# Layer 3 of a fused attention and MLP kernel: another order of its seven products, and 16 weight blocks decoded inside it

## The chip, the cores and the metric

The kernel runs on one core of one Trainium2 chip. The metric is device time in microseconds (us) of one execution.

## The reference

Three parts follow each other. The attention has 4 batches, 12 heads, 448 positions and a head size of 64, and its scores go through a capped tanh. The first MLP takes the largest of three products and multiplies it by an output matrix, all 768 wide. The second, of which the change treats the first half ("layer 3" below), is a gated product of width 1536:

```python
def _moe2_ref(x, w_gate, w_val, w_out) -> np.ndarray:
    gate = 1.0 / (1.0 + np.exp(-(x @ w_gate)))
    val = x @ w_val
    return (gate * val @ w_out).astype(np.float32)

def reference(**kwargs):
    ...
    attn_out = _attn_ref(**attn_kwargs)
    B, H, S, D = attn_out.shape
    x = np.ascontiguousarray(attn_out.transpose(0, 2, 1, 3)).reshape(B * S, H * D)
    x = _moe_ref(x=x, **moe_kwargs)
    return _moe2_ref(x=x, **moe2_kwargs)
```

The weights arrive as 8-byte floats.

## The kernel before

All weights have to be decoded from 8 bytes to 4. `decode` does this with one ScalarE operation (the absolute value of the high word) and four of VectorE: two `tensor_scalar` with one tensor operand, two `scalar_tensor_tensor` with two. A product in full precision is made of products of rounded parts: weights and inputs are split into a high and a low part (a ScalarE copy and a VectorE subtraction), and high x high, high x low and low x high are added up in PSUM.

The program runs in five stages. In the attention, 24 head pairs run one after the other (`Pair`, 6 per batch), by an order written out by hand (`PROGRAM`), in which letters also stand for steps of other work: "P", "W" and "O" advance layer 1, "d" one step of `decode_ahead`. That is a generator over 48 weight blocks (`later_weights`) with three steps a block: load 768 KB from the input and take Abs, two VectorE operations, two more and a store of 384 KB to DRAM (`ws`, `wso`, `ws3`). The blocks stand in the order in which they are used: 18 of w1, w2, w3, 6 of the output matrix, then 24 of gate and val, the blocks 10 and 11 first, then 0 to 9. What is left of layer 1 (72 products in all) and layer 2 (24) follow; they advance the decoding too, until the list is empty.

Layer 3 (`Layer3`) multiplies in the seven-product way of Strassen and Winograd: a pair of weight blocks (2j, 2j+1) and a pair of sequences give seven products, numbered 1 to 7, instead of eight. A quad (k) is one such weight pair, of gate (m = 0) or val (m = 1), for one or both of the two sequence pairs: quads 0, 1, 12 and 13 have one pair, 2 to 11 have both. Each product is 9 matmuls. `load` fetches a quad's two decoded blocks from `ws3` into `wf[k]`; `prepare`, two products ahead (AHEAD), forms sums of the weights at product 6 (four VectorE operations), and splits each weight into a ring of three places. `run` walks through the quads in `ORDER`; `ONTO` says which product goes on adding in the bank of an earlier one. `after` takes the results out: 1 is copied by ScalarE, and 6, 7, 5, 4, 3 are VectorE adds. `out` applies the sigmoid on ScalarE for a gate, or multiplies with the gate on VectorE and stores 224 KB to `us` for a val. The intermediate results live in chunks of a free list (`free`): 6 from the start and 6 more from hook (1, 5).

`hooks` are called behind product i of quad k: early ones form inputs for the second sequence pair, and from quad 2 to 11, four in each quad, `step` advances `last_weights`: rows of the last matrix are loaded (768 KB) and decoded into a tile, stored to `ws2`, loaded back as `formed` with both halves, summed in `form` (four operations) and stored to `wt2`. The last hooks fetch blocks of `us` into rooms whose old contents are no longer used, and load the first weights of layer 4 (`weights(0)`, tile w2a, three loads, the third of which takes a place of the ring). Layer 4 multiplies them. The order of instructions on each engine and queue outside the attention is set by a planner that goes by the program's order and by when it expects operands; SP issues nearly all DMAs, in one queue.

## Time and profile before

| | us |
| --- | --- |
| median of 3 runs | 1015.9 |
| the runs | 1015.47, 1015.9, 1018.31 |
| the profiled execution | 1020.39 |
| its span | 1018.5 |

A profile is one execution. It gives the busy time of each engine: PE is TensorE's matmuls, PEld its weight loads, DVE VectorE, ACT ScalarE, POOL GpSimd, SP the engine that issues DMAs. Matmuls overlap, so a full PE may still run at different paces. A name such as "ring<-w" says which tile is written from which, L541 is line 541 of the kernel, x52 a count. "<-" behind idle time names what ended it.

In the profile, times are us from the start of the span. The attention with its part of layer 1 takes the first 380 us, layer 1 and 2 run on to 551, layer 3 to 857 and layer 4 to the end.

### The profile page before, as it was taken

The page shows a single profiled execution, that of the slowest core. Times are in us where ns is not written, and L with a number is a line of the kernel's source. Part 1 is how long each engine was busy: PE and PEld are TensorE (multiplying, and loading weights), DVE is VectorE, ACT ScalarE, POOL GpSimd, SP SyncE. Part 2 cuts the span into 40 slices and gives each one's busy share as a digit, 9 for nine tenths or more (in the row PEclk, how much of TensorE's full clock was granted, in tenths as well). Part 3 has the DMA queues.
Part 4 walks back from the last instruction along what each step waited for, and adds up shares of the span by engine and source line. Part 5 has one row for each costly group of instructions (what it writes and reads, how often), then busy time and mean ns, then how long its engine had stood idle before and what let it go on. Part 6 is the DMA issues. An engine that isn't in the chain of part 4 may idle for free.

```text
span 1018.5 us, 13734 instructions
## 1 busy us (share of the span) xinstructions
PE 1001.9 (98%) x5048; PEld 837.1 (82%) x5048; DVE 753.5 (74%) x1136; ACT 500.4 (49%) x707; POOL 39.5 (4%) x49
## 2 busy tenths in 40 slices
PE   8999998999999999999999999999999999999997
PEld 3336666777788779999999999999999999999997
DVE  3988899887888886876537877686766479975661
ACT  7886676766667653444435432423241334443330
POOL 1000000000000000003630000000000000000000
PEclk9999999999999999999999999999999999999999
DMA  6774788676564569776215445454543267521331
GB/s 208 248 215 157 273 278 269 213 238 186 183 212 155 176 218 321 265 265 215 91 48 171 160 151 181 144 173 163 180 157 135 77 209 268 190 86 48 88 113 60
DMA packets 93340, 183.06 MB, mean 180 GB/s; under 512 B 33232, under 2 KB 60752, under 8 KB 92752
## 3 DMA queue, kind: packets, MB, share of 16 engines
q1 hardware_dynamic: 92832, 181.77, 53.4%
q8 instruction: 42, 0.69, 0.3%
q10 hardware_dynamic: 432, 0.33, 0.1%
q14 instruction: 34, 0.28, 0.1%
HBM read 134.48 MB, written 47.58 MB: 179 GB/s over the span
## 4 chain that ended last, share of the span: by engine, by line
PE 85%; DVE 6%; DMA 4%; ACT 3%; issue 1%; SPq 0%; DVEq 0%; ACTq 0%
PE mm L561 30%; PE mm L188 29%; PE mm L694 15%; PE pv L346 5%; PE sc L308 4%; DMA wf<-ws 1%; ACT e L313 1%; PE rest L305 1%; DMA wraw<-in_moe_w_dram 1%; ACT e L327 1%; DVE wd L131 1%; DVE wd L132 1%; PE pv L353 1%; PE pv L359 1%; DMA w2a<-ws 1%
## 5 line engine op out<-in xcount | busy, mean ns | idle before, releaser
L561 PE MATMUL mm<-part,ring 128*128 128x448 f32 x1512 | 307.4, 365 | 0.2
L561 PEld LDWEIGHTS mm<-part,ring 128*128 128x128 f32 x1512 | 283.7, 188 | 23.7 <-issue 0.9
L188 PE MATMUL mm<-x,wh 128*128 128x448 f32 x864 | 191.2, 370 | 4.8 <-ACT wh L141 4.8
L188 PEld LDWEIGHTS mm<-x,wh 128*128 128x128 f32 x864 | 161.2, 189 | 27.7 <-ACT wh L141 7.0
L188 PE MATMUL mm<-x,wl 128*128 128x448 f32 x432 | 100.3, 367 | 0.0
L141 ACT CAST wh<-wf 128x768 fp32r<-128x768 f32 x84 | 69.6, 831 | 42.3 <-DMA wf<-ws 24.0
L694 PE MATMUL mm<-w2a,u 128*128 128x384 f32 x504 | 88.5, 334 | 0.2 <-ACT w2a L668 0.2
L694 PEld LDWEIGHTS mm<-w2a,u 128*128 128x128 f32 x504 | 87.5, 188 | 0.6 <-ACT w2a L668 0.6
L188 PEld LDWEIGHTS mm<-x,wl 128*128 128x128 f32 x432 | 81.7, 189 | 7.1
L327 ACT ACTIVATE e<-e,capb 128x448 f32<-128x448 f32 (+1 forms) x96 | 86.1, 948 | 0.7
L313 ACT ACTIVATE e<-sc,tsc 128x896 f32<-128x896 f32 x72 | 70.2, 1007 | 23.3 <-PE sc L308 23.3
L142 DVE TENSOR_TENSOR wl<-wf,wh 128x768 fp32r<-128x768 f32 x72 | 68.5, 954 | 17.4 <-ACT wh L141 16.5
L694 PE MATMUL mm<-w2b,u 128*128 128x384 f32 x378 | 66.0, 334 | 0.0
L694 PEld LDWEIGHTS mm<-w2b,u 128*128 128x128 f32 x378 | 65.6, 188 | 0.0
L188 PE MATMUL mm<-h,wh 128*128 128x448 f32 x288 | 63.4, 368 | 0.0
L540 ACT CAST ring<-w 128x384 fp32r<-128x384 f32 x56 | 28.6, 510 | 69.7 <-PE mm L561 66.6
L678 ACT CAST u<-u 128x1344 fp32r<-128x1344 f32 x24 | 31.7, 1323 | 60.5 <-PE mm L694 53.0
L346 PE MATMUL pv<-e,vs 128*64 128x448 f32 x288 | 59.4, 548 | 0.0
L188 PEld LDWEIGHTS mm<-h,wh 128*128 128x128 f32 x288 | 54.1, 188 | 5.5
L126 ACT ACTIVATE wd<-wraw 128x768 f32<-128x768 f32 x48 | 43.2, 907 | 23.1 <-DMA wraw<-in_moe_w_dram 9.2
L540 ACT CAST ring<-s 128x384 fp32r<-128x384 f32 x42 | 21.5, 513 | 62.2 <-PE mm L561 59.0
L679 DVE TENSOR_TENSOR u<-u,u 128x1344 fp32r<-128x1344 f32 x24 | 37.1, 1552 | 16.6 <-ACT u L678 16.6
(132 smaller groups left out, 1208.7 us busy)
## 6 DMA issues: line engine op xcount, KB each, us to landing
wf<-ws SPq DMA_DIRECT2D x72, 384.0 KB, 3.7
ws<-wd SPq DMA_DIRECT2D x54, 384.0 KB, 2.7
wraw<-in_moe_w_dram SPq DMA_DIRECT2D x18, 768.0 KB, 5.4
wraw<-in_moe_w_out_dram SPq DMA_DIRECT2D x18, 768.0 KB, 4.8
w<-ws SPq DMA_DIRECT2D x28, 384.0 KB, 3.2
us<-temps SPq DMA_DIRECT2D x48, 224.0 KB, 2.0
u<-us SPq DMA_DIRECT2D x8, 1344.0 KB, 7.0
wraw<-in_moe_w_gate_dram SPq DMA_DIRECT2D x12, 768.0 KB, 5.6
```

What stands on the lines that cost most here:

```text
L126: nc.scalar.activation(t, high.bitcast(F32), AF.Abs)
L141: nc.scalar.copy(wh, wf)
L142: (sub or nc.gpsimd.tensor_sub)(wl, wf, f(wh))
L188: nc.tensor.matmul(ps, a[:, c, :], at(x, m, c), start=(n == 0), stop=(n == len(passes) - 1))
L308: nc.tensor.matmul(sc[:, j, :S], kk[own, c * P : (c + 1) * P], qq[own], start=(m == 0), stop=(m == last))
L313: nc.scalar.activation(e, sc[:, :w, :S], AF.Tanh, scale=tsc)
L327: nc.scalar.activation(e, e, AF.Exp, scale=1.0 if self.general else capb)
L346: nc.tensor.matmul(self.pv[0][own, :S], lhs, e, start=(c == 0), stop=(c is None))
L540: nc.scalar.copy(w[:, 0], src)
L561: nc.tensor.matmul(ps, w[:, wm, c, :], x[:, xm, c, :], start=(q == 0 and not onto), stop=(q == len(order) - 1), skip_group_check=bool(onto),)
L679: nc.vector.tensor_sub(self.part[h][1][:, :, cols], src[:, own], f(high))
L694: nc.tensor.matmul(ps, a, ww[g][:, w], start=(c == 0 and m == 0), stop=(c == KC - 1 and m == 2))
```

## The change

Three things change in layer 3, and one tuple in the attention.

- The order of the seven products becomes 1, 2, 6, 5, 7, 3, 4. Products 6, 7 and 4 go on adding in the bank of product 1, and 3 in that of 5. ScalarE copies the bank's state behind 1, 6 and 5; VectorE adds behind 2, 7 and 3; the result of 4 is read from the bank.
- Of gate and val only the blocks 10, 11, 0 and 1 (`BEFORE`) stay in the list that is decoded ahead. The 16 others are decoded inside layer 3, in halves of 384 columns, straight into the tiles from which the ring is filled, during the quad before their own. Their loads from `ws3` fall away, and so do the stores to it.
- The last weights are decoded in halves as well, into the tile in which they are summed; it is stored to `ws2` but not read back. In quads 2 to 11 seven places (three in quads 2 and 11) each take one job. Raw halves come into two places, one of which is a part of the room that gave 6 chunks to the free list and gives 4 now.
- In the attention, `self.whole` is asked where `self.alone` was. The tuple ONESX holds the pairs 0 to 5, and `alone` holds for n < 6.

```diff
+    ONESX = (0, 1, 2, 3, 4, 5)
+    BEFORE = (10, 11, 0, 1)
...
-        ORDER = (1, 6, 7, 2, 5, 4, 3)
-        ONTO = {2: 1, 3: 5}
+        ORDER = (1, 2, 6, 5, 7, 3, 4)
+        ONTO = {6: 1, 7: 1, 4: 1, 3: 5}
...
                     t = self.wpool.tile([P, KC, P], F32, tag=tag, name="w3", bufs=2)
-                    nc.sync.dma_start(out=t, in_=ws3[m, 2 * j + e])
+                    if 2 * j in BEFORE:
+                        nc.sync.dma_start(out=t, in_=ws3[m, 2 * j + e])
...
-                        ps = self.open.pop((p, onto))
+                        ps = self.open[p, onto]
...
-            if i == 1:
-                c[12] = self.new()
-                nc.scalar.copy(c[12], ps)
-            elif i == 6:
-                add(c[12], ps, c[12])
-            elif i == 7:
-                c[21] = self.new()
-                add(c[21], ps, c[12])
-            elif i == 2:
-                self.out(k, p, 0, ps)
-            elif i == 5:
-                t = self.new()
-                add(t, ps, c[21])
-                self.out(k, p, 3, t, t)
+            if i in (1, 6, 5):
+                c[i] = self.new()
+                nc.scalar.copy(c[i], ps)
             elif i == 4:
-                add(c[21], ps, c[21])
-                self.out(k, p, 2, c[21], c[21])
-            elif i == 3:
-                add(c[12], ps, c[12])
-                self.out(k, p, 1, c[12], c[12])
+                self.out(k, p, 2, ps)
+            else:
+                n, block = {2: (1, 0), 7: (5, 3), 3: (6, 1)}[i]
+                add(c[n], ps, c[n])
+                self.out(k, p, block, c[n], c[n])
...
-            for j in (*range(NF - 2, NF), *range(NF - 2)):
+            for j in BEFORE:
                 later_weights += [(cols(w, j), [P, KC, P], ws3[m, j]) for m, w in enumerate((wg, wv))]
...
+        class Decoding:
...
+            def load(self):
+                if self.begun < len(self.decodings):
+                    n = self.decodings[self.begun]
+                    raw = self.places[self.begun % 2]
+                    nc.sync.dma_start(out=raw.rearrange("p c t -> p (c t)"), in_=self.todo[n][0].bitcast(I32))
+                    self.raws[n] = raw
+                    self.begun += 1
...
+            def step(self):
+                n = self.n
+                self.n += 1
+                src, to = self.todo[n]
+                if src is None:
+                    to()
+                    return
+                decode(self.size(n), self.raws.pop(n), False)
+                self.load()
+                if n in self.sums:
+                    self.sums[n]()
...
+        def rows(c, e, h):
+            r = c + e * KC
+
+            def to():
+                if e == h == 0:
+                    formed.append(one_of(wpool, "wraw", 0, [P, 4, HALF], F32, "formed"))
+                return formed[-1][:, 2 * e + h]
+
+            return wo2[r * P : (r + 1) * P, h * HALF : (h + 1) * HALF], to
...
+        for c in range(KC):
+            last_jobs += [(rows(c, e, h), keep(c, e) if h else None) for e in range(2) for h in range(2)]
+            last_jobs.append(((None, lambda c=c: l4.form(c, formed[-1])), None))
+        for k in range(2, end - 1):
+            j, m, _ = l3.quads[k + 1]
+            now = []
+            if 2 * j not in BEFORE:
+                for e in range(2):
+                    for h in range(2):
+                        own = slice(h * HC, (h + 1) * HC)
+                        src = half((wg, wv)[m][2 * j + e][:, own])
+                        now.append(((src, lambda k=k, e=e, own=own: l3.wf[k + 1][e][:, own]), None))
+            places = [0, 1, 2, 3, 4, 5, 6] if now else [1, 3, 5]
+            now += last_jobs[:3]
+            last_jobs = last_jobs[3:]
...
+                plan.append((k, l3.ORDER[place]))
...
-            ((1, 5), lambda: [build(4, y3[:, ends], 1), l3.free.extend(temps(0))]),
-            *(((k, i), step) for k in range(2, end - 1) for i in (1, 7, 5, 3)),
+            ((1, 5), lambda: [build(4, y3[:, ends], 1), begin_decoding()]),
+            *((at, work.step) for at in plan),
```

## Rows read from the trace of the kernel before

**Rows 1.** the page: busy us, share of the span and instructions of an engine

```profile
PE 1001.9 (98%) x5048; PEld 837.1 (82%) x5048; DVE 753.5 (74%) x1136; ACT 500.4 (49%) x707; POOL 39.5 (4%) x49
```

**Rows 2.** busy time of PE, PEld, DVE, ACT, POOL by stage; granted clock, DMA

```profile
0.00:210.00 210.00, 200.65 (x945) 112.51 (x946) 175.21 (x267) 161.44 (x205) 3.25 (x25) 0.99 0.71 231
369.00:420.50 51.50, 51.50 (x255) 44.95 (x253) 39.46 (x57) 19.89 (x29) 0.00 (x0) 1.00 0.78 266
420.50:551.00 130.50, 130.50 (x632) 118.50 (x632) 80.51 (x113) 55.27 (x89) 36.27 (x24) 1.00 0.50 171
551.00:576.50 25.50, 25.38 (x125) 22.84 (x124) 25.43 (x52) 15.50 (x31) 0.00 (x0) 1.00 0.41 143
602.00:806.40 204.40, 204.40 (x1010) 189.40 (x1010) 141.09 (x252) 61.31 (x113) 0.00 (x0) 1.00 0.44 152
```

**Rows 3.** timeline (start, us, engine, line), TensorE, starts of products about 420 us

```profile
413.14 2.60 PE L188 MATMUL mm<-x,wh 128*128 128x448 f32 x12
416.79 2.59 PE L188 MATMUL mm<-x,wh 128*128 128x448 f32 x12
424.39 2.64 PE L188 MATMUL mm<-x,wh 128*128 128x448 f32 x12
428.12 2.64 PE L188 MATMUL mm<-x,wh 128*128 128x448 f32 x12
```

**Rows 4.** timeline, all engines, about 420 us; idle time before in brackets

```profile
417.70 0.96 DVE L131 SCALAR_TENSOR_TENSOR wd<-wraw,wd 128x768 int32<-128x768 int32 x1
418.57 0.61 DVE L430 TENSOR_TENSOR hm<-mm,hm 128x448 f32<-128x448 f32 x1
420.58 2.35 PEld L188 LDWEIGHTS mm<-x,wh 128*128 128x128 f32 x12 [0.36 <-ACT wh L141]
```

**Rows 5.** timeline, TensorE, the first products of layer 3

```profile
550.87 49.48 PE L561 MATMUL mm<-part,ring 128*128 128x448 f32 x240
```

**Rows 6.** line L126, 345 to 560 us: ns min/median/max, first and last start

```profile
L126 ACT ACTIVATE wd<-wraw x17: 892/910/924, 345.1 to 484.1; 128x768 f32<-128x768 f32 x17
```

**Rows 7.** groups by line of layer 3: busy us, mean ns, idle before it

```profile
L541 DVE TENSOR_TENSOR ring<-w,ring 128x384 fp32r<-128x384 f32 x52 | 28.6, 549 | 12.2 <-PE mm L561 9.5 <-ACT ring L540 2.6
L582 DVE TENSOR_TENSOR temps<-mm,temps 128x448 f32<-128x448 f32 x23 | 14.3, 623 | 20.7 <-PE mm L561 20.6
L580 ACT COPY temps<-mm 128x448 f32<-128x448 f32 x23 | 12.2, 533 | 10.9 <-PE mm L561 10.2
L102 DVE SCALAR_TENSOR_TENSOR wd<-wraw,wd 128x768 int32<-128x768 int32 x10 | 9.5, 955 | 0.2
L100 DVE TENSOR_SCALAR wd<-wd 128x768 f32<-128x768 f32 x10 | 5.6, 556 | 4.4 <-ACT wd L99 4.4
```

**Rows 8.** timeline, VectorE, in the first quad of layer 3

```profile
561.55 0.61 DVE L590 TENSOR_TENSOR temps<-mm,temps 128x448 f32<-128x448 f32 x1
```

**Rows 9.** the same view, whole run: a one-operand operation of 448 elements

```profile
L379 DVE CAST x<-xn 128x448 fp32r<-128x448 f32 x6 | 2.3, 387 | 0.0
```

**Rows 10.** timeline, VectorE, two operations that don't depend on each other

```profile
680.06 0.55 DVE L541 TENSOR_TENSOR ring<-w,ring 128x384 fp32r<-128x384 f32 x1
680.53 0.61 DVE L607 TENSOR_TENSOR temps<-temps 128x448 f32<-128x448 f32 x1
```

**Rows 11.** loads of w (384 KB) in layer 3, by tile: issue to landing

```profile
DMA to landing us min/median/max: 2.9/3.2/6.5
```

**Rows 12.** timeline, SP's queue, into layer 4

```profile
837.17 0.37 SPq L667 DMA_DIRECT2D w2a<-ws  x1
849.06 2.18 SPq L626 DMA_DIRECT2D u<-us  x2
```

**Rows 13.** DMA issues: stores of the sums, KB each, us to landing

```profile
wt<-formed SPq DMA_DIRECT2D x6, 768.0 KB, 3.9
```

**Rows 14.** chain that ended last, in order of time (start, us), into layer 4

```profile
854.57 7.23 DMA w2a<-ws
```

**Rows 15.** timeline, TensorE, into layer 4; idle time before in brackets

```profile
862.71 12.60 PE L694 MATMUL mm<-w2a,u 128*128 128x384 f32 x71 [0.25 <-ACT w2a L668]
```

More of the change, by code (lines that the diff above doesn't have):

```diff
@@ L283, in __init__ @@
             self.alone = n < NP and not general
+            self.whole = n in ONESX and not general
             self.own = general
@@ L332, in add_up @@
             nc.vector.tensor_add(self.sum, self.sum, self.e[2])
-            if self.alone:
+            if self.whole:
                 return
@@ L350, in total @@
             ld, wk, ep, pp, mm, (ident, ones, onesx, capb, tsc, kfs, vss, vts) = self.pools
[L351 to L359 removed]
+            if self.alone:
+                self.pv.append(mm.tile([P, 512], F32, tag="mm", name="pv"))
+            for j, own in enumerate(HALVES):
+                if self.whole:
+                    nc.tensor.matmul(self.pv[1][own, :S], onesx[:, j], self.e[None][:, 0], start=True, stop=False)
+            for j, own in enumerate(HALVES):
+                nc.tensor.matmul(self.pv[1][own, :S], ones[:, own], self.sum[:, j], start=not self.whole, stop=True)
         def finish(self):
@@ L626, in fetch @@
             nc.sync.dma_start(out=t, in_=us[self.pairs[e][i], half * KC : (half + 1) * KC].rearrange("c p s -> p c s"))
-        def load_sums(self, c):
-            t = two(self.wpool, "wraw", [P, 4, HALF], F32, "formed")
-            for e in range(2):
-                nc.sync.dma_start(out=t[:, 2 * e : 2 * e + 2], in_=ws2[e * KC + c].rearrange("p (a f) -> p a f", a=2))
-            return t
         def form(self, c, t):
@@ L970, in compute @@
         l4 = Layer4(pairs, rooms, mm, wpool, sm)
-        def last_weights():
-            for c in range(KC):
-                for r in (c, KC + c):
-                    raw = raw_bits(wpool, wo2[r * P : (r + 1) * P, :], [P, DM])
-                    yield
-                    wf = decode(two(wpool, "wf", [P, DM], F32, "wd"), raw)
-                    nc.sync.dma_start(out=ws2[r], in_=wf)
-                    yield
-                t = l4.load_sums(c)
-                yield
-                l4.form(c, t)
-                yield
@@ L986, in compute, with __init__, start, size @@
-        steps = last_weights()
         tops, ends = slice(0, HC), slice(HC, KC)
         end = len(l3.quads) - 1
-        def step():
-            next(steps, None)
+        class Decoding:
+            def __init__(self, todo, sums):
+                self.todo, self.sums, self.raws, self.begun = todo, sums, {}, 0
+                self.decodings = [n for n, (src, _) in enumerate(todo) if src is not None]
+            def load(self):
[5 more added lines that the diff above has]
+                    self.begun += 1
+            def start(self, places):
+                self.places, self.n, self.early = places, 0, None
+                self.load()
+                self.load()
+            def size(self, n):
+                to = self.todo[n][1]()
+                to = to.rearrange("p c f -> p (c f)") if len(to.shape) == 3 else to
+                nc.scalar.activation(to, self.raws[n][..., 1].bitcast(F32), AF.Abs)
+                return to
+            def step(self):
[6 more added lines that the diff above has]
+                decode(self.size(n), self.raws.pop(n), False)
+                self.load()
+                if n in self.sums:
+                    self.sums[n]()
@@ new lines, in half, with keep, store @@
+        def half(src):
+            return src.rearrange("p c f -> p (c f)")
+        formed = []
+        def rows(c, e, h):
[5 more added lines that the diff above has]
+            return wo2[r * P : (r + 1) * P, h * HALF : (h + 1) * HALF], to
+        def keep(c, e):
+            def store():
+                nc.sync.dma_start(out=ws2[c + e * KC].rearrange("p (a f) -> p a f", a=2), in_=formed[-1][:, 2 * e : 2 * e + 2])
+            return store
@@ new lines, in compute @@
+        todo, plan, sums, last_jobs = [], [], {}, []
+        for c in range(KC):
[13 more added lines that the diff above has]
+            last_jobs = last_jobs[3:]
+            for place, (job, done) in zip(places, now):
+                if done:
+                    sums[len(todo)] = done
+                todo.append(job)
+                plan.append((k, l3.ORDER[place]))
@@ L993, in compute, with begin_decoding @@
+        work = Decoding(todo, sums)
+        def begin_decoding():
+            t = rooms.chunks(0, "temps")
+            l3.free.extend(t[:, c] for c in range(HC + 1))
+            size = 2 * HALF
+            spare = t[:, HC + 1 :].rearrange("p c s -> p (c s)")[:, :size]
+            other = one_of(wpool, "wf", 0, [P, size], F32, "raw")
+            work.start([x.bitcast(I32).rearrange("p (c t) -> p c t", t=2) for x in (other, spare)])
         at_ = [
```

9 lines of the change are left out of this document (removed).

## The prediction

> **What bounds the kernel now.** I read the page's busy shares first, then the busy time by stage, then TensorE's own timeline where the change works. TensorE is busy 98% of the span, VectorE 74% [rows 1]. By stage [rows 2] the only stretch in which TensorE is not full is the first 210 us, the attention that comes before most of layer 1: 200.65 of 210. From there to the end TensorE is full: 130.50 of 130.50 in the end of layer 1 and layer 2, 204.40 of 204.40 in the eight middle quads of layer 3. Busy TensorE is not yet TensorE at its peak, so I looked at its pace, which the starts of its products show: a product of layer 1 or 2 is 18 matmuls, and from start to start it takes 416.79 - 413.14 = 3.65 us before 420 us, and 428.12 - 424.39 = 3.73 us after [rows 3]. The clock is granted in full on both sides [rows 2]. The slower pace begins with a gap: at 420.58 the weights of the next product are late by 0.36 us, because a VectorE operation that they stand behind (L430) ran behind a decode operation, L131 [rows 4], and it lasts to the first product of layer 3 at 550.87 [rows 5]. So TensorE sets the time everywhere that the change touches, and a gain can come only from gaps and from this pace; a loss comes wherever TensorE is no longer fed.
>
> **The sum is made against the profiled execution**, 1020.39 us with a span of 1018.5, so 1.9 lie around the span. The runs shown have a median of 1015.9, 4.5 below it, and differ among themselves by 2.84. I carry each term over to the median and say where that changes it. About 0.3%, 3.0 us, is what a measurement of this kernel can tell from no change.
>
> **Part 1, 16 decodes leave the planned list.** The list gives 3 steps for each of 48 blocks; the programs of the pairs spend 91 of these steps up to pair 21 and 12 more in pairs 22 and 23, so with 32 blocks (96 steps) everything before the last step of pair 22 is as it was. So the first 210 us, where TensorE waits, stay as they are. The last 17 blocks of the list begin between 345.1 and 484.1 us [rows 6]; 16 of these go, with their stores and later reloads, and TensorE is full there. What they can give back is the gap at 420.58 and the pace behind it. From 420.58 to 550.87 there are 35 products: 130.29 us, and 35 x 3.65 = 127.75 at the faster pace. That is 2.5 us, and with the gap itself (the product before began at 416.79, so 420.44 was due: 0.14) 2.7 us. Bounds: -2.7 when no gap comes in its place; +1 when the stretch from 369 to 420 us, now at the faster pace, falls into the slower (14 products of 0.075). For the profiled execution I take -2.7. The three runs shown differ by 2.84, which is about this term, so the median may have the faster pace already; for the median I take half, -1.3.
>
> **Part 2, four products in one bank.** A quad (one weight block pair, both sequence pairs) had 10 adds and 2 ScalarE copies on its way out of PSUM, and has 6 and 6 after. VectorE loses 4 x 0.62 = 2.5 us a quad, ScalarE gains 4 x 0.53 = 2.1 us [rows 7]. No matmul goes. New are four waits of TensorE on readers of a bank it goes on adding to: the copy behind product 1 before 6, behind 6 before 7, the add behind 7 before 4, the copy behind 5 before 3. In a quad with both pairs at least three products of 9 matmuls (1.82 us each) lie between, 5.5 us for an operation of 0.53 to 0.62: nothing. In the four quads with a single pair only one product lies between, 1.82 us. There the profile shows what such a spot costs: in the first quad the add L590 begins at 561.55 and ends at 562.17 [rows 8], while its bank was due for product 3 at 550.87 + 6 x 1.82 = 561.8: a gap of about 0.4. VectorE is full there, 25.43 of 25.50 [rows 2], and loses 2 adds in each such quad. Bounds for the two quads at the start: -0.4 (the gap goes) and four spots x 0.4 = +1.6. I take +0.3, nearest to the row of one gap. Behind the copies on ScalarE the ring copies of the weights are queued, which have two products of slack.
>
> **Part 3, decoding inside layer 3.** In quads 3 to 10 (602 to 806 us) there come 4 half blocks for the next quad and 3 of the last weights' jobs, of which on average 2.4 are half blocks and 0.6 the forming of sums. A whole decode is 2 x 0.556 + 2 x 0.955 = 3.02 us of VectorE; for a half, the two one-operand operations are 0.353 each (0.387 at 448 elements and 0.556 at 768, so 0.53 ns an element), and the two others 0.549 as the ring's subtraction of 384: 1.80 [rows 7, 9]. A quad then holds: 7 ring subtractions 3.84, four sums 2.2, 6 adds 3.7, so 9.8, with 8 products of the gate 14.7 in every second quad; decoding 6.4 x 1.80 + 0.6 x 4 x 0.55 = 12.8. Sums: 22.6 and 27.5, mean 25.1, against 14 x 1.825 = 25.55 of TensorE. That is an upper bound, as operations without a dependence start before the one ahead has ended: L541 at 680.06 lasts 0.55, L607 starts 0.47 behind [rows 10]. With 0.08 off for each but half of the decode's: 20.5 and 24.7, mean 22.6. So VectorE comes to between 88 and 98% of these 204 us; now it is 141.09 of 204.40, 69% [rows 2].
>
> A rule of the Trainium skill speaks against this edit (its page VectorE: DVE Perf Modes, section The DRAIN you can't avoid): the next operation starts only when the pipe of the one ahead is empty. The trace differs, with 0.47 behind an operation of 0.55. By that rule the load would be the 25.1 of whole durations, by the trace 22.6.
>
> The load is hidden as long as the lag of VectorE stays inside what covers it. A ring slot is filled two products ahead: 7.3 us less 0.51 and 0.55, so 6.2 us. The decoded halves are first read 3 to 5 places behind their decode, 11 us or more. A quad with gate products lags by at most 27.5 - 25.55 = 2.0 and the next makes it good by 2.9. So I take 0 for this part.
>
> The raw halves come into two places, 6.4 in 25.55 us, so each place may turn in 8.0 us. It needs 3.2 for a load of 384 KB (2.9 to 6.5) [rows 11] with 0.4 to issue it on SP [rows 12], at most 0.53 for ScalarE's Abs and 1.8 of decode: 5.9, up to 9.2 with the slowest load. The load waits on SP for the decode ahead of it; queued behind it are the stores of the gate products, which come from the same VectorE, in the same order, and nobody near waits for them. ws2 is no longer read back for the sums (12 loads less), which costs nothing else: the store stays. The sums now lie in one place instead of two: behind a forming (2.2) its store takes 0.4 and 3.9 [rows 13], 6.5 in all, and the next half is due after 3.65. So it comes 2.8 late at the four points at which a forming is followed by a half in the next place of the order (quads 3, 5, 8, 10). That lies inside the 6.2 if nothing else lags. Bounds of this part: 0 and, with none of the four covered, +11. The pool of free chunks falls from 12 to 10; at most 10 are alive at once, and the copy behind product 6 then takes a chunk whose store left one product earlier. That wait falls on ScalarE, with three products of cover.
>
> **Part 4, the way into layer 4.** The order 1, 2, 6, 5, 7, 3, 4 moves the last uses of two rooms: part 6 of the second pair is free one product later (1.82 us), part 7 two later. The two fetches of 1344 KB, issued now at 849.06 and behind it [rows 12], move by as much; the third load of the first weights, issued at 854.57 and landed 7.23 later, still waits for the fifth product of the last quad, and comes to stand beside or behind the second fetch. Now it costs TensorE 0.25 at 862.71 [rows 14, 15]. Bounds: -0.25 (the queue is shorter by a fetch) and +1.8 (all land one product later). I take +0.8, the middle, as no row is nearer to either end.
>
> **The rest** costs nothing: in the attention, the totals issue the same matmuls in the same order, as the new tuple names the pairs that the old condition names. Layer 4 is as it was.
>
> Sum for the profiled execution: 1020.4 - 2.7 + 0.3 + 0 + 0.8 = 1018.8. For the median: 1015.9 - 1.3 + 0.3 + 0 + 0.8 = 1015.7. That is my forecast: **no difference that can be told**. Its own range is 1013 to 1019.
>
> **Rivals.** (a) VectorE becomes the bound of layer 3. For it: 25.1 of 25.55 by whole durations, and its idle waits. Now each decode of last weights waits 0.44 for Abs (4.4 in 10) [rows 7]; 6.4 of them would add 2.8 a quad. By overlapped starts 22.6 + 2.8 = 25.4 still fits; by whole durations 27.9 is 2.3 over, 19 in eight quads. Against it: an engine that lags finds its inputs ready, so such waits shrink as it lags. It decides from the point at which load and waits pass 25.55. I price it between the two, at +8: 1024. The DRAIN rule of the skill named above would lead here. (b) The pace: a gap at the start of layer 3 leaves TensorE in the slower one. 1512 matmuls are 84 times 18, 84 x 0.075 = 6.3: 1022. For it, the four new tight spots; against it, its pace in layer 3 now is the faster one although two gaps lie ahead of it. (c) Faster: the median has the slower pace, all of part 1 comes through, and the gaps of parts 2 and 4 go: 1015.9 - 2.7 - 0.4 - 0.25 = 1012.5. Against it: the spread of the runs shown, which suggests that the faster pace is in the median. (d) The change does not do what it says: the decodes it takes out held nothing up. Then part 1 is 0 and the time 1017, inside the forecast's own range.
>
> **How the numbers follow.** Forecast with (d) 0.62, (a) 0.19, (b) 0.11, (c) 0.08. Slower by over 0.3% (above 1019) are (a) and (b) but for the mild ends of (a), 0.29 in all; faster (below 1012.9) is (c) with 0.08; the rest, 0.63, is no change. For 8 in 10 the range starts at (c)'s 1012.5 and reaches to the price of (a), 1024; beyond it are the upper half of (a) and little else. The bounds of the parts (-2.7 to +1, -0.4 to +1.6, 0 to +11, -0.25 to +1.8) add to -3.4 and +15; that all stand at their upper ends at once is left out.
>
> **What would show it.** Right: TensorE full from 210 us on, VectorE at 88 to 98% in the quads of layer 3, 3.65 us a product up to layer 3. Wrong in part 3: waits of TensorE for ring subtractions, or for an add or a copy of its bank, from quad 3 on, and layer 3 longer than 306.5 us. Wrong in part 4: the first product of layer 4 waits for w2a or the fetched blocks by over 2 us. Wrong in part 1: a gap between 369 and 551 us, or the pace of 3.73 without one. The prediction as a whole is wrong if the first 210 us change.

## The result, and the profile after

The changed kernel takes 1020.79 us in the median of 20 executions (1017.72 to 1030.62), the kernel before, timed beside it, 1016.0 (20 executions, 1012.86 to 1021.58). The ratio is 1.0055, interval 1.0036 to 1.0074: slower by 4.8 us. The forecast was no difference, 1015.7 us with an own range of 1013 to 1019: the time lies above that, though inside the wider range given for 8 in 10, 1012.5 to 1024. The profiled executions hide the loss: 1020.61 after, near its median, and 1020.39 before, 4.4 above its median. They differ in where the time goes.

| us from the start of the span | before | after |
| --- | --- | --- |
| first matmul of layer 2 | 461.6 | 459.9 |
| of layer 3 | 550.9 | 547.4 |
| of layer 4, behind the last of layer 3 | 858.5 | 857.1 |
| the last matmul | 1011.6 | 1011.9 |
| layer 3 | 307.6 | 309.7 |
| layer 4 | 153.1 | 154.8 |

So in these two executions 3.5 us are gained before layer 3 and lost again in layers 3 and 4. The profiled execution of the kernel before was a long one; whether most of its executions have such 3.5 us to gain is asked below. First, the busy time of the changed kernel by stage (stretch, its length, busy us and count of PE, PEld, DVE, ACT and POOL, granted clock, share and rate of the DMA):

```profile
0.00:210.00 210.00, 200.62 (x945) 111.56 (x946) 175.54 (x268) 161.53 (x205) 3.23 (x25) 0.99 0.72 231
...
420.50:547.40 126.90, 126.90 (x628) 117.62 (x627) 46.36 (x76) 46.78 (x77) 35.63 (x24) 1.00 0.26 78
...
598.40:804.00 205.60, 204.34 (x1005) 188.04 (x1004) 172.65 (x378) 87.78 (x180) 0.00 (x0) 1.00 0.55 169
```

Against [rows 2], the first 210 us are as they were (200.65 of TensorE before). The end of layer 1 and layer 2 stay full. In quads 3 to 10 VectorE is busy for 84% of the time, and TensorE, full before, misses 1.3 us by busy time (2.3 by the starts of its matmuls, below). The chain of work that ended last shows what it waits for (start, duration, what):

```profile
379.58 167.99 PE mm L190 x828
547.58 120.47 PE mm L563 x594
...
679.24 3.09 DMA raw<-in_moe_w_gate_dram
...
686.22 0.56 ACT w L982
...
756.14 3.87 DMA temps<-in_moe_w_out_dram
...
794.84 4.57 DMA temps<-in_moe_w_out_dram
...
801.43 38.59 PE mm L563 x189
...
854.09 9.61 DMA w2a<-ws
863.72 0.84 ACT w2a L652
```

Up to 668 us the chain is TensorE alone. From 679 to 801 it alternates between raw loads, Abs (L982) and decodes, although TensorE is nearly full: the work there has no slack left. How that reaches TensorE is seen in the timeline of all engines about 767 us (start, duration, engine, line, what, in brackets the idle time before and what ended it):

```profile
760.00 0.33 SPq L970 DMA_DIRECT2D raw<-in_moe_w_out_dram  x1
...
763.03 0.33 SPq L970 DMA_DIRECT2D temps<-in_moe_w_val_dram  x1
763.08 0.56 ACT L982 ACTIVATE formed<-raw 128x384 f32<-128x384 f32 x1 [1.66 <-DMA raw<-in_moe_w_out_dram]
...
764.96 0.35 DVE L102 TENSOR_SCALAR formed<-formed 128x384 f32<-128x384 f32 x1
...
766.45 0.54 ACT L982 ACTIVATE w<-temps 128x384 f32<-128x384 f32 x1 [2.81 <-DMA temps<-in_moe_w_val_dram]
767.02 0.36 DVE L102 TENSOR_SCALAR w<-w 128x384 f32<-128x384 f32 x1 [0.73 <-ACT w L982]
767.14 0.53 ACT L582 COPY temps<-mm 128x448 f32<-128x448 f32 x1
767.30 0.55 DVE L105 SCALAR_TENSOR_TENSOR formed<-raw,formed 128x384 int32<-128x384 int32 x1
...
767.72 2.30 PE L563 MATMUL mm<-part,ring 128*128 128x448 f32 x10 [0.92 <-ACT temps L582]
...
767.93 0.33 SPq L970 DMA_DIRECT2D raw<-in_moe_w_val_dram  x1
...
769.10 0.55 DVE L105 SCALAR_TENSOR_TENSOR w<-temps,w 128x384 int32<-128x384 int32 x1
769.57 0.55 DVE L534 TENSOR_TENSOR s<-w 128x384 f32<-128x384 f32 x1
769.73 0.33 SPq L970 DMA_DIRECT2D temps<-in_moe_w_val_dram  x1
```

ScalarE sits for 2.81 us in front of an Abs whose raw half has not landed. Behind it in the queue stands L582, the copy of a bank's state, and TensorE waits for that copy before it may add on in the bank: it is the copy behind product 6 of quad 9, whose last matmul had begun at 760.70, and product 7 cannot begin without it. The distance from matmul to matmul is 1278 ns where 203 is usual.

The half that was missing is not late for its reader. Counted through the list of jobs, the load at 763.03 is a half of val for quad 11. In the program its decode stands behind product 1 of quad 10, which begins at 778.8; the planner put its Abs 12 us earlier, ahead of a copy of quad 9. It is late only for that place in ScalarE's queue.

For this order the two raw places turn too slowly: the place "temps" is loaded at 756.14, 763.03 and 769.73, every 6.9 and 6.7 us; "raw" at 760.00 and 767.93, 7.9. Of these 7.9 the load takes 3.05, Abs 0.56, then the half waits 1.3 until VectorE has done the sums and ring steps queued ahead of it (764.96), and its decode is spread over 2.9 us, because the first operation of the next half stands ahead of its last step and itself waits 0.73 for its Abs. By the starts of neighbouring matmuls, four gaps between 761 and 802 us, two in quad 9 and two in quad 10, add to 2.3 us.

The second place of the loss is the way into layer 4 (the same timeline, there):

```profile
833.38 0.37 SPq L617 DMA_DIRECT2D u<-us  x1
...
838.88 1.56 DVE L668 TENSOR_TENSOR u<-u 128x1344 f32<-128x1344 f32 x1 [0.93 <-DMA u<-us]
...
841.76 0.62 DVE L587 TENSOR_TENSOR temps<-mm,temps 128x448 f32<-128x448 f32 x1
...
842.43 0.87 PE L563 MATMUL mm<-part,ring 128*128 128x448 f32 x3 [0.61 <-DVE temps L587]
...
850.03 0.36 SPq L617 DMA_DIRECT2D u<-us  x1
853.68 0.36 SPq L617 DMA_DIRECT2D u<-us  x1
854.09 0.54 SPq L651 DMA_DIRECT2D w2a<-ws  x1
857.47 2.54 ACT L662 CAST u<-u 128x1344 fp32r<-128x1344 f32 x2 [5.07 <-DMA u<-us]
863.72 0.83 ACT L652 CAST w2a<-w2a 128x768 fp32r<-128x768 f32 x1 [3.71 <-DMA w2a<-ws]
```

In quad 12, a quad with one pair, the add behind product 7 (L587) stands on VectorE behind L668, a combination of fetched blocks for layer 4 (the sum of blocks 21 and 22 of the first pair), which waits for a fetch. TensorE has one product of cover there and loses 0.9. In the kernel before, the same fetch and the same sum (L684 there) come 7 and 8 us later, behind the adds of quad 12 and not before one that TensorE waits for:

```profile
840.57 0.37 SPq L626 DMA_DIRECT2D u<-us  x1
...
847.05 1.56 DVE L684 TENSOR_TENSOR u<-u 128x1344 f32<-128x1344 f32 x1 [0.49 <-DMA u<-us]
```

So the new order has this block ready earlier, 2.7 us into quad 12 instead of 8.1, and the loss is that the planner then puts the sum in front of the add. Then the third load of w2a is issued at 854.09, behind two fetches, and takes 9.61 to land (7.23 in [rows 14]); the first product of layer 4 waits 1.56 instead of 0.25 [rows 15].

### The profile page after: what moved, and what is told of

Read it like the earlier page. It is cut to its first block, busy times and chain, and to the rows that moved or that the text cites. A ratio compares the mean times of both kernels' runs of the same rounds, so it can differ in the third digit from the quotient of the medians.

```text
span 1018.7 us, 13810 instructions
## 1 busy us (share of the span) xinstructions
PE 999.3 (98%) x5048; PEld 835.8 (82%) x5048; DVE 730.4 (72%) x1200; ACT 524.3 (51%) x783; POOL 38.9 (4%) x49
## 4 chain that ended last, share of the span: by engine, by line
PE 72%; DVE 11%; DMA 9%; ACT 3%; issue 2%; SPq 2%; DVEq 0%; ACTq 0%
PE mm L190 29%; PE mm L563 17%; PE mm L678 14%; PE pv L349 5%; PE sc L311 4%; DMA wraw<-in_moe_w_dram 2%; PE pv L360 1%; DVE temps L587 1%; PE rest L308 1%; DMA temps<-in_moe_w_out_dram 1%; DVE temps L598 1%; DMA wf<-ws 1%; DVE wd L133 1%; DMA w2a<-ws 1%; DVE wd L134 1%
## 5 line engine op out<-in xcount | busy, mean ns | idle before, releaser
L144 DVE TENSOR_TENSOR wl<-wf,wh 128x768 fp32r<-128x768 f32 x72 | 68.6, 953 | 25.8 <-ACT wh L143 25.1
L431 DVE TENSOR_TENSOR hm<-mm,hm 128x448 f32<-128x448 f32 x48 | 29.8, 621 | 34.1 <-PE mm L190 33.6
L587 DVE TENSOR_TENSOR temps<-mm,temps 128x448 f32<-128x448 f32 x72 | 44.3, 617 | 6.6 <-PE mm L563 6.3
L582 ACT COPY temps<-mm 128x448 f32<-128x448 f32 x72 | 37.8, 530 | 20.9 <-PE mm L563 11.4
```

The costliest lines, as they stand in the source:

```text
L144: (sub or nc.gpsimd.tensor_sub)(wl, wf, f(wh))
L582: nc.scalar.copy(c[i], ps)
L587: add(c[n], ps, c[n])
```

## The experiments

The theory after this reading has two parts. **Places**: two raw places turn too slowly for the order in which the planner put the decodes, and the copies behind Abs on ScalarE pass this to TensorE (2.3 us). **Way in**: the new order, with the fetches where they were, delays quad 12 and the third weights of layer 4 (about 2 us more than before). Rivals: VectorE's load, and the pace of TensorE.

### A third raw place

Room 0 gives up four chunks more (two small tiles take their part in the free list), and three raw halves are under way instead of two.

```diff
-                    raw = self.places[self.begun % 2]
+                    raw = self.places[self.begun % 3]
...
+                self.load()
...
-            l3.free.extend(t[:, c] for c in range(HC + 1))
+            l3.free.extend(t[:, c] for c in range(2))
+            l3.free.extend(sm.tile([P, S], F32, tag="hm", name="temps") for _ in range(2))
```

> The changed kernel with three places for raw halves instead of two, and three loads begun ahead; the third place is made of two chunks of the room, for which two tiles of another pool go to the free list, so the free list keeps its 10 chunks. The changed kernel has a median of 1020.8, and its profiled layer 3 holds 3.2 us of gaps of TensorE, all from 761 us on. Theory 'places': a place turns too slowly (load, Abs, decode, next load), the decoding runs late against TensorE, and ScalarE and VectorE hand this on. Then a third place takes these gaps away: about 1017.8, and no gap of TensorE between quads 3 and 11. Rival 'load of VectorE': its work, not the places, is what lags; then the gaps stay within 1 us and the time at 1020 to 1021. Rival 'order of the queue': the bank copies stand behind Abs on ScalarE, which waits for a load wherever it stands; then gaps stay, at other products, and the time falls by less than 1.5.

1017.51 us (ratio 1.0008, 0.9997 to 1.002). The chain of this kernel:

```profile
548.73 290.03 PE mm L563 x1431
841.50 11.43 PE mm L563 x54
853.36 9.20 DMA w2a<-ws
...
863.46 6.60 PE mm L678 x35
```

Layer 3 is TensorE alone for 1431 matmuls, at 202.7 ns each; the raw loads are gone from the chain, with the same operations on VectorE. In the stretch of quads 3 to 10 TensorE is full again, although VectorE is busier than in the changed kernel (176.23 us for 172.65):

```profile
598.40:804.00 205.60, 205.60 (x1016) 190.51 (x1016) 176.23 (x381) 93.13 (x185) 0.00 (x0) 1.00 0.55 171
```

So the places made the gaps in the middle of layer 3, and VectorE's load did not. (They lie in quads 9 and 10 of the numbering from 0; expectations below call them those of quads 8 and 9.) What is left stands at 841.50 and 863.46. That the time fell by the expected 3 us is less sure: a second timing of this kernel, in the last section, came out 4.0 us above the kernel before. Whether copies set ahead of the Abs on ScalarE would do as well was not tested.

### Fetching later, alone and with the third place

```diff
-            ((end, 2), lambda: l4.fetch("21", 1, 9)),
+            ((end, 3), lambda: l4.fetch("21", 1, 9)),
```

> The changed kernel with one hook moved: the last fetch of the second pair (1344 KB) is asked for behind product 3 of the last quad instead of behind product 2, so that the third load of layer 4's first weights stands ahead of it on the queue. In the changed kernel's profile that load takes 9.6 us behind the fetch, and TensorE waits 1.9 us for it. Theory 'queue': the load lands 3 to 4 us after its issue and this wait goes, about 1019.3; the rest of the loss stays. Rival 'bytes': the other fetch, still ahead, holds the DMA engines as long, the load lands no more than 1 us earlier and the time stays at 1020.8.

1018.82 us (1.0025, 1.0011 to 1.0039). The profiled execution took 1028.52: from 381 us to the gap at 850 its matmuls follow each other every 206.7 ns instead of 202.7. The first product of layer 4 still waits 1.47, so the wait that this edit was to remove is there as before. The time is near the 1019.3 of theory 'queue', but not by that theory's way; what made the median 2 us shorter is not shown.

> Both edits at once: three places and the late fetch. If 'places' and 'queue' hold and the two parts add up, 1016.3, the kernel before within 1 us. If the load of VectorE is the cause, 1019.3. If neither, 1020.8.

1017.38 us (1.001, 0.9995 to 1.0024), as with the third place alone. The loads of w2a now land in 5.2 us at most, but the cast of the third stands behind the casts of a fetched block on ScalarE, which had waited 5.02 for that fetch; TensorE waits 1.24. The wait has passed from one queue to another, and the 1016.3 of the two theories together was missed.

### The order of the products alone

Into the kernel before goes the new order with its `after`, and nothing else.

```diff
-        ORDER = (1, 6, 7, 2, 5, 4, 3)
-        ONTO = {2: 1, 3: 5}
+        ORDER = (1, 2, 6, 5, 7, 3, 4)
+        ONTO = {6: 1, 7: 1, 4: 1, 3: 5}
```

> The kernel before with the new order of the products alone (copies by ScalarE, four products in a bank); all 48 blocks are decoded ahead and the last weights as before. If the loss comes from the decoding inside layer 3 and from the way into layer 4, the order alone costs the wait at layer 4, 1.3 us: 1017.3, and layer 3 has no gaps beyond its first quads. Rival 'bank waits': the copies and adds that TensorE waits for cost the time themselves; then gaps like those of the changed kernel stand in layer 3 and the time is 1019 or more.

1021.17 us (1.0049, 1.0029 to 1.0069): the order alone costs what the whole change costs. That is neither the 1017.3 expected nor the rival's gaps: its timeline shows no gap in quads 2 to 11, and these two places:

```profile
835.29 1.56 DVE L673 TENSOR_TENSOR u<-u 128x1344 f32<-128x1344 f32 x1 [1.06 <-DMA u<-us]
...
838.18 0.62 DVE L585 TENSOR_TENSOR temps<-mm,temps 128x448 f32<-128x448 f32 x1
...
838.85 14.86 PE L561 MATMUL mm<-part,ring 128*128 128x448 f32 x72 [0.73 <-DVE temps L585]
...
861.53 8.78 PE L683 MATMUL mm<-w2a,u 128*128 128x384 f32 x40 [2.08 <-ACT w2a L657]
```

Behind the second gap the busy time by stretch (columns as above) shows a lower granted clock:

```profile
856.00:859.40 3.40, 3.40 (x20) 3.13 (x19) 2.68 (x2) 0.83 (x1) 0.00 (x0) 1.00 1.04 380
861.50:864.50 3.00, 2.97 (x9) 2.97 (x10) 3.00 (x3) 0.83 (x1) 0.00 (x0) 0.52 0.50 118
```

0.52 is the level of 1.2 GHz: nine matmuls follow each other at 320 ns instead of 173, another 1.3 us. Waits of 0.9 and 2.25, by the starts of matmuls, come with this to some 4 us more than the 0.8 that the kernel before loses from quad 12 on.

### All blocks decoded ahead, the rest of the change kept

```diff
-    BEFORE = (10, 11, 0, 1)
+    BEFORE = (10, 11, 0, 1, 2, 3, 4, 5, 6, 7, 8, 9)
```

> The changed kernel with all 24 blocks of gate and val in the list that is decoded ahead, as before; the new order of products and the halves of the last weights stay in layer 3. The order alone came out at 1021.2, the changed kernel with three places at 1017.5. Theory 'two losses': the decoding of the 16 blocks with two places costs the gaps in quads 3 to 11 (2.3 us in the changed kernel's profile), the order costs the rest, in quads 12 and 13 and at layer 4. Then this kernel has no gaps in quads 2 to 11, and a time of 1018.5 to 1020. Rival 'decoding alone': 1016.5. Rival 'order alone': 1021, with the gaps of the changed kernel at the end of layer 3 and none before.

1022.78 us (1.0053, 1.0031 to 1.0075), above the 1018.5 to 1020 expected, and not the faster kernel that a layer 3 freed of 16 decodes would give. Fewer halves remain, but the mechanism does too, once, as ScalarE's timeline shows:

```profile
710.43 0.56 ACT L982 ACTIVATE formed<-temps 128x384 f32<-128x384 f32 x1 [2.61 <-DMA temps<-in_moe_w_out_dram]
710.89 0.52 ACT L582 COPY temps<-mm 128x448 f32<-128x448 f32 x1
```

TensorE resumes at 711.46, 0.3 us late. In this execution its matmuls had followed each other at a slower pace since 555 us, 206.7 ns instead of 202.7, and the faster came back with that gap; the slower stretch alone costs 3.0 us. The way in costs 3.1 in gaps, as in the changed kernel.

### Two fetches moved behind the weights

Blocks 21 of both pairs are asked for behind `weights(0)`. Three kernels: with the third place; with the order alone; in the kernel before, there at (end, 3).

```diff
-            ((end - 2, 7), lambda: l4.fetch("21", 0, 12)),
...
-            ((end, 2), lambda: l4.fetch("21", 1, 9)),
...
+            ((end, 4), lambda: [l4.fetch("21", 0, 12), l4.fetch("21", 1, 9)]),
```

> Three places for raw halves, and two fetches of 1344 KB moved to the last hook of layer 3, behind the first weights of layer 4: the one whose subtraction ran on VectorE in quad 12 ahead of the add that TensorE waited for (0.9 us in the kernel with three places), and the one ahead of the third weight load. Theory 'queues into layer 4': both gaps, 0.9 to 1.2 and 1.1 to 1.6 us, go or fall under 0.5, and the time is 1015 to 1016, the kernel before or a little less. Rival 'bytes': with three fetches behind each other the later ones come late for layer 4, a gap of 1 to 3 us stands at its fourth tile or its second product, and the time stays at 1017.5 or above. Rival 'tight cover': the add behind product 7 has one product of cover in quad 12 and stays late whatever VectorE does before it; then only the second gap goes, 1016.3.

1017.66 us (1.000, 0.9981 to 1.0018), no better than the third place alone. The planner put the first fetch back where its room comes free, so the gap in quad 12 stayed (0.7 us), and the casts on ScalarE still stood ahead of the third w2a (wait 1.68).

> The kernel before with the new order of products alone, and the same two fetches moved to the last hook. The order alone measured 1021.2, with a wait of 2.4 us for the third weight load, a slower pace behind it and a gap of 0.9 in quad 12. If the order costs its time only by these queues, 1016.5 to 1017.5 and both gaps under 0.5. If the order costs time elsewhere (single pair quads at the start, copies), it stays at 1019 or more.

1019.49 us (1.0015, 0.999 to 1.0041); the interval doesn't part it from the order alone. In its profile L673 waits so long for a fetch that the gap in quad 12 is 2.2 us, with matmuls of 373 ns behind it at a granted clock of 0.56.

> The kernel before with the two fetches moved behind the first weights of layer 4, nothing else. Its own gaps there are 0.7 us in all. If the move is good by itself, 1015.5; if it only undoes what the new order did, 1016.2; if the fetches come late for layer 4, 1017 or more. It is the control for the two others.

1014.43 us (0.998, 0.9956 to 1.0004), the lowest median of all, though the interval touches 1. Its chain runs through layer 3 without a stop from 558 us on and waits 0.4 at layer 4:

```profile
558.30 292.20 PE mm L561 x1440
850.56 6.78 DMA w2a<-ws
857.36 0.85 ACT w2a L668
858.25 11.89 PE mm L694 x67
```

In the order before, product 6 is the second and 7 the third of a quad, so the rooms of their inputs come free early in the last quad, and the blocks that layer 4 needs first can be there in time. This is read from the program; no run takes it apart.

### The way in mended, with the third place

The rooms of two fetches are exchanged, so that block 22 of the first pair cannot be fetched, and its sum not be asked for, before the last quad; 11 of the second pair is fetched behind product 6.

```diff
-            ((end - 1, 6), lambda: l4.fetch("22", 0, 11)),
+            ((end - 1, 6), lambda: l4.fetch("21", 1, 11)),
...
-            ((end, 7), lambda: l4.fetch("11", 1, 8)),
-            ((end, 2), lambda: l4.fetch("21", 1, 9)),
+            ((end, 6), lambda: l4.fetch("11", 1, 8)),
...
+            ((end, 4), lambda: l4.fetch("22", 0, 9)),
```

> The changed kernel with the third raw place, and with the rooms of two fetches exchanged: 21 of the second pair (needed late, but complete early) goes into room 11, 22 of the first pair into room 9, which comes free inside the last quad; and 11 of the second pair is fetched behind product 6 instead of 7. So the sum of 21 and 22 of the first pair cannot be asked for before about 860 us, and nothing in quad 12 stands behind a fetch. Theory (the loss of the change is the raw places plus the way into layer 4): gaps in quads 2 to 13 below 0.3 us together, the wait at the first product of layer 4 below 1, last matmul near 1008, time 1014 to 1016, two to three us below the version with the third place alone (1017.5). Rival (the way in is bound by what the queues have to carry whatever their order, so that the wait only moves): 1017 to 1018 as with the third place alone.

> The same as the run before it, but all 12 blocks of gate and val decoded ahead again, as in the kernel before; the last weights alone are decoded in layer 3. This leaves only the place of the 16 decodes as the difference between the two. If decoding them ahead costs what the prediction says of the profiled execution (gap near 420 us and the slower pace of 3.73 us behind it), this run is up to 2.7 us longer than the other, 1016 to 1019; if it costs nothing in the median, the two agree within 1 us. The rival for the earlier run with all blocks ahead (1022.8), that layer 3 itself is slower with them because of their loads, would give 1019 or more here, with gaps in quads 2 to 11.

The first did in the trace half of what was meant: no gap is left from 381 us to layer 4 in any of its five profiles, whose executions took 1016.1 to 1017.9 us. So the sum that waited for its fetch made the gap of quad 12. But at layer 4 the wait stays, by its timeline because the casts of the fetched block stand ahead of that of w2a:

```profile
854.94 2.53 ACT L662 CAST u<-u 128x1344 fp32r<-128x1344 f32 x2 [5.19 <-DMA u<-us]
...
857.37 0.83 ACT L652 CAST w2a<-w2a 128x768 fp32r<-128x768 f32 x1
...
858.25 12.06 PE L678 MATMUL mm<-w2a,u 128*128 128x384 f32 x68 [1.50 <-ACT w2a L652]
```

And its median is 1023.3 (1.0059, 1.0033 to 1.0085), from two groups: four executions from 1014.9 to 1017.9, eight from 1021.3 to 1027.6. With all blocks decoded ahead it was 1019.1 (1.0033, 1.0011 to 1.0056), two of twelve above 1021. Neither theory gave this.

### Single executions with a profile, and the timing repeated

> The changed kernel once more, one execution with a profile. If the gaps in quads 8 and 9 come from the order of the queues, they stand here again within 5 us of where they stood (761 and 768 us), 1.5 to 2.5 us in sum, with a copy behind an Abs on ScalarE; if they were an accident of that execution, they are gone. The pace (203 or 207 ns from matmul to matmul) may differ.

This execution of the changed kernel took 1026.02 us, and the gaps of quads 9 and 10 are not there. Its chain:

```profile
379.37 171.31 PE mm L190 x828
550.68 295.75 PE mm L563 x1431
848.64 11.23 PE mm L563 x54
```

The 828 matmuls of layers 1 and 2 take 171.31 where they took 167.99, the 1431 of layer 3 295.75 where the version with the third place took 290.03: 206.9 and 206.7 ns instead of 202.9 and 202.7. At this pace TensorE is slow enough for the two places to keep up; the late fetch with its two places, which ran at 206.7 ns from 381 us on, has no gap in quads 2 to 11 either.

> The changed kernel once more. If its gaps in quads 8 and 9 belong to the faster pace: an execution that enters layer 3 at 202.7 ns shows 1.5 to 2.5 us of gaps between 700 and 805 us and a time of 1017 to 1022; one that enters at 206.7 ns shows none and a time above 1024.

The changed kernel again, 1018.48 us, at the faster pace: 2.2 us of gaps between 765 and 801 us, with the copy L582 at 765.24 behind an Abs that had waited 2.58, and 1.0 in quad 12. The gaps belong to the order of the queues and to the faster pace, as expected.

> The kernel before once more, one execution with a profile. If the slower pace behind the gap at 420 us is settled by the program, layer 1 and 2 again run at 3.73 us a product from 420 to 551 us; if it is a matter of chance, they run here at 3.65 in part or throughout, and layer 3 begins up to 2.7 us earlier than 550.9.

The kernel before, 1024.46 us: slower pace from 381 to 444 us, faster to 576, slower through the rest of layer 3 (5.5 us). The pace differs from execution to execution of one kernel, and the 2.5 us that the prediction read from one execution were one draw of it.

> The version with the third place and the mended way into layer 4 once more, one execution with a profile. If the upper group is the slower pace held from 380 us on: a time of 1014 to 1018 goes with 202.7 ns from matmul to matmul, a time of 1022 to 1028 with 206.7 ns up to about 860 us and with layer 4 starting near 863 instead of 854.5. If it is a loss at the way into layer 4: a time above 1021 goes with layer 4 starting near 854.5 and with a wait or slower matmuls behind that.

1016.1 us, and 1017.51 and 1017.53 in two further executions, all at the faster pace. An execution of the upper group was not caught.

> The version with the third place and the mended way into layer 4, timed again. If the upper group belongs to it, again about half of the executions or more lie above 1021 us, with a median of 1021 or more; if not, the executions lie at 1014 to 1019 with a median of 1016, one to two us below the version with the third place alone.

> The version with the third place alone, timed beside it. If the slower pace is entered by chance at 380 us, where the two versions are alike, both show about the same share of executions above 1021 us; if this one has none again (1015 to 1020, median 1017.5) while the other has many, the group belongs to what differs between them, the way into layer 4.

The mended way in again: 1020.99 us (1.0061, 1.0028 to 1.0094), four of nine above 1021. The third place alone beside it: 1018.86 (1.0045, 1.0016 to 1.0074), four of twelve above 1021, up to 1029.8, where its first timing had none. So the group isn't a property of the way in. It may belong to the chip: the first timing of the third place ran on another chip than the second, and no run tests this. That the group is the slower pace is argued, not shown, for these two kernels: held through layers 1 to 3 it would cost 9 us (3.3 in layers 1 and 2, 5.7 in layer 3), and in the first timing of the mended way in the means of the groups lie 8 us apart; the two other executions that were caught above 1025 (1026.02 and 1028.52) had that pace from 381 us to quad 12; and none of the five profiles without gaps left the pace that it entered.

The traces can be compared without the pace. The time from the first matmul of layer 3 to the last matmul of the program, in the profiles that ran these at the faster pace:

| kernel | us, one per profile |
| --- | --- |
| before (its first 11 us at the slower pace, 0.2) | 460.7 |
| changed | 464.5, 464.0 |
| with the third place | 462.3, 462.0 |
| with the third place and the mended way in | 460.6 to 461.1 (five) |

The change loses 3.3 to 3.8 us here. The third place gives about 2.1 of them back, the mended way in 1.2 more; with both the traces stand within 0.6 of the kernel before.

## Why the prediction was wrong, step by step

**Part 1, the decodes taken off the list**: the profile did what was said. No gap stands between 381 and 547 us in any profile of the change, and the profiled execution gained the 2.7 us (layer 3 begins 3.5 earlier; the rest lies before 380 us). What failed is the carrying over to the median, for which half was taken, 1.3. The text took the slower pace for a consequence of the gap near 420 us. A gap at 418 to 452 us stands in six of the seven profiles of kernels with all blocks decoded ahead, but the slower pace came in with it only in the one that the prediction read. Of the seven profiles of kernels with all blocks decoded ahead, three had the slower pace in layers 1 and 2 (2.5, 1.2 and 2.2 us); of the thirteen without, two had it (3.3 each). That is 0.8 against 0.5 on average: by these few profiles the median had next to nothing to give back.

**Part 3, taken at 0: the largest term that was missed, 2.2 to 2.3 us.** Its first half held: VectorE has 84% of load, 21.6 us a quad, below the 88 to 98% that were given (by its own rule, 0.08 off for each, the lower sum comes to 22.2, not 22.6); a half's one-operand operation takes 0.356 (0.353 was estimated), and rival (a) did not come. By whole durations VectorE would have been at 98% (25.1 of 25.55); here L105 at 769.10 lasts 0.55, and an operation that does not depend on it (L534) begins 0.47 later. The Trainium skill (VectorE: DVE Perf Modes, section The DRAIN you can't avoid), which the prediction cited for whole durations, itself adds that a next operation that is not held starts earlier. The 0.47 is such an earlier start, so the trace does not speak against that section as a whole. The step that failed is "each place may turn in 8.0 us" with its "It needs" of 5.9. The need was a sum of durations without the queues between them: the turns took 6.7 to 7.9, in the longest 1.3 us of waiting for VectorE and a decode drawn out from 1.8 to 2.9. And the 8.0 was an average over 6.4 halves; a quad whose seven jobs are all halves, as quad 9 is, has 2 x 25.55 / 7 = 7.3. The cover was looked for in the wrong queue, too: the decoded halves did have their 11 us and more, but the late load held up ScalarE, where a bank copy stood behind Abs. The sign set for this, a wait for a copy of a bank from quad 3 on, did come; the other, layer 3 longer than 306.5 us, says nothing, since it took 307.6 before.

**Part 2, +0.3**: "In the four quads with a single pair only one product lies between" named the right spots, and then only the two quads at the start were costed. Those give nothing (0.07 in gaps, 0.46 before), as the lower bound allowed; the cost came at quad 12, 0.6 us more than before in quads 12 and 13. Behind the copies the text named the ring copies that wait, and not Abs ahead of them.

**Part 4, +0.8 with an upper bound of 1.8**: the direction and the mechanism were right, the third load of w2a came late. The first product of layer 4 lost 1.5 us more than before in gaps, within the bounds but nearly twice the middle that was taken; the order alone, where the wait is 2.25, fell to the lower clock behind it. Here the size was wrong, not the step.

The terms as the traces give them: 0 instead of -1.3, 2.2 instead of 0, quads 0, 1, 12 and 13 +0.2 net instead of +0.3, +1.5 instead of +0.8. This sums to 3.9 of the 4.8. The rest is left open; five of 22 executions of the changed kernel lie above 1025 and one of 129 of the kernel before, and the slower pace may be why. Rival (b), the pace in layer 3, is not what made the profiled execution, which stands near the median at the faster pace. At the upper end the slower pace was seen once, at 1026.02, and there it held from 380 us on and did not come from a gap at the start of layer 3; for the 1028.38 and 1030.62 of the timing itself it is argued. The way of rival (b) itself shows in the kernel with all blocks decoded ahead: a gap at 554.9, and the slower pace behind it to 711 us.

## What to carry to other kernels

Price a buffer's turn by its queues, not by its operations: on an in-order engine, an operation that waits for a DMA holds up whatever stands behind it, and if that is a copy out of PSUM, a late load stops TensorE without VectorE being full. Cost a reordering at its last stage: the rooms that it frees later are those that the next stage must fetch into, and what it has ready earlier can be queued in front of work that TensorE waits for. And read a small gain in one profiled execution against a second execution before it enters the sum.

## What the runs showed of the hardware

At the full granted clock, matmuls of 448 columns with their weight loads follow each other at one of two paces, 202.7 or 206.7 ns. A pace stayed over up to 2350 matmuls, and changes of it stand at gaps, from 0.05 us up: [rows 3, 5] show one such change, and in the executions above both directions occur. One change stands at no gap: in the order alone with the two fetches moved, the pace goes from 202.7 to 206.7 ns at 432 us. Many gaps change nothing. The first gap behind the attention, at 380 us, is the same in all kernels (469 or 470 ns from matmul to matmul), and either pace follows it. A kernel with no gap behind it kept its pace for 470 us in every profile, a difference of 9.1 us, while the two profiles of the kernel before changed it at gaps. What decides the pace, and why some timings of a kernel have many executions at the upper end and others none stayed open.

Three gaps at the end of layer 3 and the start of layer 4, of 2.0 to 2.25 us, were followed by some ten matmuls at a granted clock of 0.52 to 0.57, the level of 1.2 GHz in part of the stretch (320 ns for 384 columns, 373 for 448). Behind the gap of 1.7 us in the changed kernel, and behind one of 1.84 with the third place and the two fetches moved, it stayed at 1.00. Each of the three gaps cost another 1.4 to 1.7 us in this way.
